# Gate weights and gate logits: one batch or row block in each column quadrant, and transposes in place of stack matmuls

## The chip, the cores and the metric

The kernel runs on one core of a Trainium2 chip. The metric is the time of one execution on the device, in microseconds; for the kernel before, three runs were taken (752.5, 754.86 and 754.75, median 754.75).

## The reference

Dilated and windowed attention over 4 batches of 576 positions gives 2304 tokens of 512 numbers. Then a gated product, and then eight experts, between which a greedy routing divides the tokens:

```python
x = attention(q, k, v)                       # (2304, 512)
x = (((x @ w1) * (x @ w2)) @ w3) @ w_out     # FF = 1024 inside, D = 512 outside
logits = x @ w_gate                          # (2304, 8)
for idx in argsort(-logits.flatten()):       # best (token, expert) pairs first
    # a token that has no place yet goes to the expert, while it has fewer than 288
    ...
for e in range(8):
    out[mask_e] = relu(x[mask_e] @ w1_e[e]) @ w2_e[e]
```

All in float32. Large products are made of three passes over a high and a low part; the logits, on whose order the routing depends, are plain fp32 products.

## The kernel before

**Stages.** The order of the work is written out by hand: Python generators are advanced against each other, and each engine runs its instructions in the order in which they were written. First comes attention, interleaved with the loading of weights. Then `moe(b)` (L398) makes G = (x w1) * (x w2) for each batch b of 576 tokens: in groups of 12 passes (L414 to L416) for 256 or 320 tokens, ScalarE copies one product out (L419) and VectorE multiplies it by the other (L420). G[b] is two tiles of 4 x 128 features by 576 tokens.

**Gate weights.** While `moe(3)` runs, `gates()` (L326) is advanced by one step at each half group. It computes WG = w3 (w_out w_gate), which turns the logits into G times WG, so that the routing need not wait for x. In step c it transposes four 128 x 128 pieces of w_out on TensorE (`turn`, L333; one bank, tag "tr"), ScalarE copies them out, and in the next step four matmuls (`gate`, L343) multiply them by four 128-row pieces of w_gate, one in each column quadrant of the array, that is 32 of its 128 columns. Each quadrant thus holds a quarter of one sum (a partial sum over 128 of 512 features). After every four steps the bank is copied to `ts`, and four stack matmuls (L363) with `ts` as the stationary operand and a 128 x 8 matrix of ones (`C_STK`) as the moving one add the four quadrants and turn the result round; VectorE copies that to `TS` (L364). The bank of tag "rt" exists once, so the next accumulator waits for that copy. Then follows the product with w3 (L372), for which SP fetches the pieces in two sets (`fetch_w3`).

**Logits.** Behind `moe(3)` the logits are made (L803 to L820). In each of eight turns u half a batch (288 tokens, `HT`) is multiplied by WG: 8 matmuls, feature blocks 0 to 3 and then 4 to 7, four column quadrants in turn, each with the sum over two of the eight blocks. ScalarE copies the bank to `lt` (L813), and 18 stack matmuls (L817), as soon as 128 tokens are ready, add the quadrants and turn 128 tokens onto the partitions. One VectorE copy (L820) puts all 2304 x 8 logits into `L`. Ahead of the last stack matmuls one unit of the next product is issued (`next(fill)`).

**Routing and what fills it.** From `L` on the routing (`routing`, L587) is a long chain on VectorE with small matmuls (L744) in between. `filler()` (L1035) puts units of other work on TensorE in between: first the product w3 w_out (`make_w`, L514; a unit is three matmuls, L523 to L525, counted as 680 ns), then x2 (`make_x2`), then the experts. A written-out pace (L1040 to L1046) says how many units stand ahead of each routing step. With block c of x2, from c = 11, `w_split` is called, which splits one expert weight into its high and low part on ScalarE and on VectorE, GpSimd (L122) or a GpSimd DMA; `gsplit` makes GpSimd DMAs too.

Of the kernel before, what the change touches and what calls it, by code (L numbers as in the profile page):

```python
# [9 lines left out]
F32 = mybir.dt.float32  # L10
# [3 lines left out]
AF = mybir.ActivationFunctionType  # L14
# [5 lines left out]
B, S = 4, 576  # L20
N, D, FF, E, CAP = 2304, 512, 1024, 8, 288
QB, KB, NB = 64, 96, 9
HT = 288
HEAD = 256
NC = N // 128
# [4 lines left out]
C_ID, C_STK = 0, 128  # L30
# [55 lines left out]
def body(tc, qk_d, v_d, ke_d, ve_d, msk_d, cst_d, tri_d, w1_d, w2_d, w3_d, wo_d, wg_d, e1_d, e2_d, out):  # L86
    nc = tc.nc
    stacks = {}

    def pool(name, **kw):  # L90
        stacks[name] = ExitStack()
        return stacks[name].enter_context(tc.tile_pool(name=name, bufs=1, **kw))
# [8 lines left out]
    bank = lambda shape, tag, dt=F32: ps.tile(shape, dt, tag=tag, name="ps_" + tag,  # L101
                                              bufs={"ab": 4, "h": 2, "tr": 1, "rt": 1}[tag])
    mm = nc.tensor.matmul
    act = nc.scalar.activation
    dve = nc.vector
# [4 lines left out]
    def slot(i, shape, dt, name):  # L110
        return xp.tile(shape, dt, tag=f"s{i}", name=name, bufs=1)
# [31 lines left out]
    C = cst.tile([128, C_END], F32, name="C")  # L143
    ident = C[:, C_ID:C_ID + 128]
# [148 lines left out]
    got3, narrowed, pre, placed = {}, {}, {}, [0]  # L293
# [28 lines left out]
    TS = pm.tile([128, 512], F32, tag="xr", name="TS", bufs=1)  # L322
    WG = TS[:, :256].rearrange("p (m e) -> p m e", m=8)
    TS = TS[:, 256:].rearrange("p (m e) -> p m e", m=8)

    def gates():  # L326
        wts, accs = [], []
        wg32 = p3.tile([128, 4, 32], F32, name="wg32", bufs=1)
        dve.memset(wg32, 0.0)
        dve.tensor_copy(wg32[:, :, 0:8], wg)  # L330
        dve.memset(TS, 0.0)

        def turn(c):  # L333
            w = narrowed["wo", c // 2]
            t = bank([128, 4, 128], "tr")
            for i in range(4):
                n0 = 512 * (c % 2) + 128 * i
                nc.tensor.transpose(t[:, i, :], w[:, n0:n0 + 128], ident)
            wt = p3.tile([128, 4, 128], F32, tag="wt", name="wt", bufs=1)
            act(wt, t, AF.Copy)  # L340
            wts.append(wt)

        def gate(c):  # L343

            if c % 4 == 0:
                accs.append(bank([128, 4, 128], "rt"))
            wt = wts.pop()
            for i in range(4):
                mm(accs[-1][32 * i:32 * i + 32, c % 4, :], wg32[:, i, :], wt[:, i, :], start=True, stop=True)

        for c in range(9):
            if c:
                gate(c - 1)
            if c in (4, 8):
                ts = p3.tile([128, 4, 128], F32, tag="ts", name="ts", bufs=1)
                act(ts, accs[-1], AF.Copy)
            if c < 8:
                turn(c)
            yield
            if c in (4, 8):  # L360
                o = bank([128, 4, 8], "rt")
                for i in range(4):
                    mm(o[:, i, :], ts[:, i, :], C[:, C_STK:C_STK + 8], start=True, stop=True)  # L363
                dve.tensor_copy(TS[:, c - 4:c, 0:8], o)  # L364
        yield

        acc = bank([128, 2, 128], "rt")
        for a, ms in enumerate(((4, 5, 6, 7), (0, 1, 2, 3))):
            ws = [narrowed["w3", m] for m in ms]
            for k in range(8):  # L370
                for q, w in enumerate(ws):
                    mm(acc[32 * q:32 * q + 32, a, :], TS[:, k, :], w[:, 128 * k:128 * k + 128],  # L372
                       start=(k == 0), stop=(k == 7))
                if k % 2:
                    yield
            if ms[0]:
                fetch_w3(0)
                for _ in range(3):
                    yield
        wt = p3.tile([128, 4, 128], F32, tag="wt", name="wt", bufs=1)[:, :2]  # L380
        act(wt, acc, AF.Copy)
        yield
        t = bank([128, 2, 128], "tr")
        for a in range(2):
            nc.tensor.transpose(t[:, a, :], wt[:, a, :], ident)
        for a in range(2):
            dve.tensor_copy(WG[:, 4 - 4 * a:8 - 4 * a, :], t[:, a, :].rearrange("p (q e) -> p q e", q=4))

    def fetch_w3(m):
        x = p3.tile([128, 2, 1024], F32, tag="S", name="S", bufs=1)  # L390
        for i in range(4):
            fetch(("w3", m + i), x[:, i] if i < 2 else pm.tile([128, 1024], F32, tag="f", name="f", bufs=2))


    G = {}
    L = cst.tile([128, E, NC], F32, name="L")
# [58 lines left out]
    nxt, i = 0, 0  # L455
# [8 lines left out]
    for b in range(B):  # L464
        if b == 3:
            stacks.pop("pa").close()
            p2 = pool("p2")
            p3 = pool("p3")
            for i in range(2):
                x = p2.tile([128, 2, 1024], F32, tag=f"P{i}", name="wo", bufs=1)  # L470
                for n in range(2):
                    fetch(("wo", 2 * i + n), x[:, n])
            fetch_w3(4)
            making_wg = gates()
# [59 lines left out]
    def make_x2():  # L534

        yield from make_w()
        todo = []

        def xout(c, a):
            late = c - (NC - ONE)  # L540
            if late >= 0:
                if not X1:
                    X1.extend(wtile("wb"))
                h, l = [x[:, D * late:D * late + D] for x in X1]
                act(h, a, AF.Copy)
                dve.tensor_tensor(l, a, f32(h), op=OP.subtract)
            r = pm.tile([128, D], F32, tag="xr", name="xr", bufs=1) if late < 1 else rows0[0][:, 3 * D:4 * D]
            act(r, a, AF.Copy)
            nc.scalar.dma_start(x2_d[128 * c:128 * c + 128, :], r)

        def mul(a, g, f, cols):
            h, l = g
            wh, wl = [x[:, f % 2, cols] for x in Wx[f // 2]]
            mm(a, h[:, f, :], wh, start=(f == 0), stop=False)  # L554
            mm(a, h[:, f, :], wl, start=False, stop=False)  # L555
            mm(a, l[:, f, :], wh, start=False, stop=(f == 7))  # L556

        for c in range(NC):
            if c + 2 < NC:
                gsplit(c + 2)  # L560
            if c >= 11:
                w_split()
            if c >= 10:
                w_gather()
            a = bank([128, D], "ab")
            for f in range(8):
                mul(a, GS[c], f, slice(0, D))
                if f == 1 and todo:
                    xout(*todo.pop())
                if f == 2 and c == NC - ONE:  # L570
                    while 0 not in lists:
                        yield 0
                    first_rows()
                yield 680
            todo.append((c, a))
        yield from first_in(lambda: xout(*todo.pop()))
# [223 lines left out]
    route = routing()  # L800
    next(route)
    fill = make_x2()
    lt = slot(3, [128, N], F32, "lt")  # L803
    lo = bank([128, NC, E], "tr")
    c = 0
    for u in range(2 * B + 1):
        if u < 2 * B:
            lg = bank([128, HT], "h")
            for i in range(2):
                for q in range(4):  # L810
                    mm(lg[32 * q:32 * q + 32], WG[:, 4 * i + q, :],
                       G[u // 2][i][:, q, HT * (u % 2):HT * (u % 2) + HT], start=(i == 0), stop=(i == 1))
            act(lt[:, HT * u:HT * u + HT], lg, AF.Copy)  # L813
        else:
            next(fill)
        while u and 128 * (c + 1) <= HT * (u if u == 2 * B else u - 1):
            mm(lo[:, c, :], lt[:, 128 * c:128 * c + 128], C[:, C_STK:C_STK + 8],  # L817
               start=True, stop=True)
            c += 1
    dve.tensor_copy(L, lo.rearrange("p c e -> p e c"))  # L820


    pieces = [(k, n, i) for k in range(E)
              for n, i in ([(1, 0), (1, 1), (2, 0), (2, 1), (1, 2), (2, 2), (1, 3), (2, 3)] if k == 0 else
# [210 lines left out]
    def filler():  # L1035
        yield from fill_x2
        phase[0] = 1
        yield from experts()

    fill_x2, fill = fill, filler()  # L1040
# [67 lines left out]
```

## Time and profile before

| | |
|---|---|
| median of three runs | 754.75 us |
| profiled execution | 752.74 us, span 751.0 us |
| mean granted clock of TensorE | 0.997 |
| TensorE (PE) busy | 720.0 us, 96% |
| weight loads (PEld) | 651.9 us, 87% |
| VectorE (DVE) | 411.0 us, 55% |
| ScalarE (ACT) | 355.7 us, 47% |
| GpSimd (POOL) | 298.8 us, 40% |
| chain that ended last | PE 75%, DVE 9%, issue 6%, ACT 4%, POOL 3% |

Busy times are sums over one execution. A matmul's duration includes its way through the array, and matmuls overlap, so the time of a run of matmuls is the distance of the starts, not the sum of the durations. The chain that ended last goes back from the last instruction to what released it, and so on; its shares tell on which engines the length hangs.

### The profile page before, as it was taken

To read this page: it belongs to the slowest core of one execution; us is meant where nothing else is said; L and a number is where in the kernel's file an instruction comes from. 1 tells how busy PE (TensorE), PEld (TensorE's weight loads), DVE (VectorE), ACT (ScalarE), POOL (GpSimd) and SP (SyncE) were. 2 spreads that over 40 slices of the span, in tenths; PEclk is the share of its full clock that TensorE was granted. 3 is DMA by queue.
4 is the path that set the end of the run, shared out by engine and by line. 5 is a ranking of instruction groups with operands and counts; after the bars stand their busy time and mean duration, and the time that the engine had idled before them with its cause. 6 is when DMAs were issued, how large, how long until landed. Compare 5 with 4: busy or idle time off the path is not lost.

```text
span 751.0 us, 17097 instructions
## 1 busy us (share of the span) xinstructions
PE 720.0 (96%) x6606; PEld 651.9 (87%) x6606; DVE 411.0 (55%) x1360; ACT 355.7 (47%) x833; POOL 298.8 (40%) x357
## 2 busy tenths in 40 slices
PE   5799999999999999999999999999999999999997
PEld 3589999899999988877778787779999999999996
DVE  4987778832322100137787668677788762124321
ACT  5674544444442212422345356426575566665432
POOL 1876211101010002815354456334475574763531
PEclk9999999999999999999999999999999999999999
DMA  8984899832200503011669789976887978996511
GB/s 313 338 251 125 297 348 320 277 108 68 74 28 1 224 2 113 29 36 57 112 82 138 119 123 197 200 224 164 232 235 219 273 213 240 263 272 216 156 33 33
DMA packets 57410, 126.74 MB, mean 169 GB/s; under 512 B 9584, under 2 KB 27120, under 8 KB 54768
## 3 DMA queue, kind: packets, MB, share of 16 engines
q1 hardware_dynamic: 27088, 89.46, 35.7%
q0 software_dynamic: 27648, 31.46, 24.1%
q10 hardware_dynamic: 2592, 4.72, 1.8%
q8 instruction: 52, 0.85, 0.5%
q14 instruction: 30, 0.25, 0.1%
HBM read 87.87 MB, written 15.73 MB: 138 GB/s over the span
## 4 chain that ended last, share of the span: by engine, by line
PE 75%; DVE 9%; issue 6%; ACT 4%; POOL 3%; DMA 2%; SPq 1%; POOLq 0%; DVEq 0%; ACTq 0%
PE ps_ab L414 9%; PE ps_ab L415 8%; PE ps_ab L416 8%; PE ps_ab L554 4%; PE ps_ab L555 3%; PE ps_ab L556 3%; PE ps_h L935 3%; PE ps_h L936 3%; PE ps_h L937 3%; PE ps_ab L959 3%; PE ps_ab L961 3%; PE ps_ab L960 3%; PE ps_rt L744 2%; PE ps_rt L223 2%; PE ps_ab L523 2%
## 5 line engine op out<-in xcount | busy, mean ns | idle before, releaser
L420 DVE TENSOR_TENSOR g<-a,ps_ab 128x256 f32<-128x256 f32 (+1 forms) x64 | 28.9, 452 | 137.4 <-PE ps_ab L416 131.7
L204 POOL TENSOR_TENSOR p<-p,sm 128x384 f32<-128x384 f32 x36 | 38.9, 1080 | 151.2 <-ACT p L197 75.9
L414 PE MATMUL ps_ab<-x,wah 128*128 128x256 f32 (+1 forms) x256 | 78.7, 307 | 0.0
L414 PE MATMUL ps_ab<-x,wbh 128*128 128x256 f32 (+1 forms) x256 | 78.5, 307 | 0.0
L439 POOL DMA_DIRECT2D wbl<-g x40 | 52.2, 1706 | 63.2 <-ACT wbl L437 53.2
L416 PE MATMUL ps_ab<-x,wal 128*128 128x256 f32 (+1 forms) x256 | 76.2, 298 | 0.0
L415 PE MATMUL ps_ab<-x,wah 128*128 128x256 f32 (+1 forms) x256 | 76.2, 298 | 0.0
L959 PE MATMUL ps_ab<-hh,w 128*128 128x288 f32 x248 | 75.9, 306 | 0.0
L416 PE MATMUL ps_ab<-x,wbl 128*128 128x256 f32 (+1 forms) x256 | 75.7, 296 | 0.0
L415 PE MATMUL ps_ab<-x,wbh 128*128 128x256 f32 (+1 forms) x256 | 75.7, 296 | 0.0
L961 PE MATMUL ps_ab<-hh,w 128*128 128x288 f32 x248 | 73.0, 294 | 0.0
L960 PE MATMUL ps_ab<-hl,w 128*128 128x288 f32 x248 | 72.9, 294 | 0.0
L419 ACT ACTIVATE a<-ps_ab 128x256 f32<-128x256 f32 (+1 forms) x64 | 26.1, 408 | 97.3 <-PE ps_ab L416 97.3
L197 ACT ACTIVATE p<-p,sm 128x96 f32<-128x96 f32 x144 | 52.0, 363 | 37.1 <-DVE sm L190 37.1
L948 DVE SCALAR_TENSOR_TENSOR hl<-ps_h,hh 128x288 fp32r<-128x288 f32 x62 | 28.2, 455 | 68.7 <-ACT hh L947 68.7
L947 ACT ACTIVATE hh<-ps_h 128x288 fp32r<-128x288 f32 x62 | 25.5, 412 | 84.5 <-PE ps_h L937 84.5
L554 PE MATMUL ps_ab<-Wx,wbh 128*128 128x512 f32 x144 | 60.2, 418 | 0.0
L555 PE MATMUL ps_ab<-Wx,wbh 128*128 128x512 f32 x144 | 56.8, 394 | 0.0
L556 PE MATMUL ps_ab<-Wx,wbl 128*128 128x512 f32 x144 | 56.7, 394 | 0.0
L414 PEld LDWEIGHTS ps_ab<-x,wah 128*128 128x128 f32 x256 | 49.0, 191 | 2.6 <-issue 1.0
L414 PEld LDWEIGHTS ps_ab<-x,wbh 128*128 128x128 f32 x256 | 48.4, 189 | 3.1 <-issue 1.0
L416 PEld LDWEIGHTS ps_ab<-x,wal 128*128 128x128 f32 x256 | 49.0, 192 | 0.0
(272 smaller groups left out, 2123.7 us busy)
## 6 DMA issues: line engine op xcount, KB each, us to landing
w<-w_dram SPq DMA_DIRECT2D x16, 1024.0 KB, 8.1
est<-e_dram SPq DMA_DIRECT2D x31, 512.0 KB, 5.0
qk<-qk_dram SPq DMA_DIRECT2D x36, 320.0 KB, 5.1
yt<-e_dram SPq DMA_DIRECT2D x22, 512.0 KB, 5.2
wbl<-g POOLq DMA_DIRECT2D x32, 256.0 KB, 6.3
v<-v_dram SPq DMA_DIRECT2D x36, 192.0 KB, 4.3
kept<-f SPq DMA_DIRECT2D x12, 512.0 KB, 4.0
w<-est POOLq DMA_DIRECT2D x12, 512.0 KB, 6.5
```

Source lines behind the costliest of these rows:

```text
L197: act(p[:, i, :], p[:, i, :], AF.Exp, bias=sm[:, 1, i:i + 1], scale=-1.0, accum_out=sm[:, 2, i:i + 1])
L204: nc.gpsimd.tensor_tensor(p, p, sm[:, 3, :, None].to_broadcast([128, 4, KB]), op=OP.mult)
L414: mm(a, wh[:, k, fs], xh[:, k, ts], start=(k == 0), stop=False)
L415: mm(a, wh[:, k, fs], xl[:, k, ts], start=False, stop=False)
L416: mm(a, wl[:, k, fs], xh[:, k, ts], start=False, stop=(k == 3))
L439: nc.gpsimd.dma_start(x, src, accum_op=OP.add)
L554: mm(a, h[:, f, :], wh, start=(f == 0), stop=False)
L555: mm(a, h[:, f, :], wl, start=False, stop=False)
L556: mm(a, l[:, f, :], wh, start=False, stop=(f == 7))
L959: mm(y, wh[:, f % 2, ds_], h, start=(f == 0), stop=False)
L960: mm(y, wh[:, f % 2, ds_], l, start=False, stop=False)
L961: mm(y, wl[:, f % 2, ds_], h, start=False, stop=(f == end))
```

## The change

The gate weights: one accumulator holds all eight row blocks. In step r (group g, feature block i) the four transposed pieces are of four row blocks and one feature block; quadrant q of the array takes row block q, and the sum over the four feature blocks is made by accumulating over four steps. At the end there are one copy of 256 columns, two plain transposes and one VectorE copy. The logits: quadrant b takes batch b, and the sum over the eight feature blocks is accumulated in place, for tokens 0 to 287 of all batches and then 288 to 575. ScalarE copies each quadrant to its place in `lt`, which is now 128 x 640; batches 1 and 3 stand 64 columns further right, so that five 128 x 128 transposes turn all tokens as the routing wants them. GpSimd fills the columns left over with zeros, three units of the next product stand ahead of the transposes, and five VectorE copies go to `L`.

```diff
@@ -324,44 +324,40 @@
     TS = TS[:, 256:].rearrange("p (m e) -> p m e", m=8)
 
     def gates():
-        wts, accs = [], []
         wg32 = p3.tile([128, 4, 32], F32, name="wg32", bufs=1)
         dve.memset(wg32, 0.0)
         dve.tensor_copy(wg32[:, :, 0:8], wg)
         dve.memset(TS, 0.0)
-
-        def turn(c):
-            w = narrowed["wo", c // 2]
+        acc = bank([128, 2, 128], "rt")
+
+        def turn(r):
+            g, i = divmod(r, 4)
             t = bank([128, 4, 128], "tr")
-            for i in range(4):
-                n0 = 512 * (c % 2) + 128 * i
-                nc.tensor.transpose(t[:, i, :], w[:, n0:n0 + 128], ident)
+            for q in range(4):
+                w = narrowed["wo", 2 * g + q // 2]
+                n0 = 512 * (q % 2) + 128 * i
+                nc.tensor.transpose(t[:, q, :], w[:, n0:n0 + 128], ident)
             wt = p3.tile([128, 4, 128], F32, tag="wt", name="wt", bufs=1)
             act(wt, t, AF.Copy)
-            wts.append(wt)
-
-        def gate(c):
-
-            if c % 4 == 0:
-                accs.append(bank([128, 4, 128], "rt"))
-            wt = wts.pop()
-            for i in range(4):
-                mm(accs[-1][32 * i:32 * i + 32, c % 4, :], wg32[:, i, :], wt[:, i, :], start=True, stop=True)
-
-        for c in range(9):
-            if c:
-                gate(c - 1)
-            if c in (4, 8):
-                ts = p3.tile([128, 4, 128], F32, tag="ts", name="ts", bufs=1)
-                act(ts, accs[-1], AF.Copy)
-            if c < 8:
-                turn(c)
+            return wt
+
+        def gate(r, wt):
+            g, i = divmod(r, 4)
+            for q in range(4):
+                mm(acc[32 * q:32 * q + 32, g, :], wg32[:, i, :], wt[:, q, :], start=(i == 0), stop=(i == 3))
+
+        for r in range(8):
+            wt = turn(r)
             yield
-            if c in (4, 8):
-                o = bank([128, 4, 8], "rt")
-                for i in range(4):
-                    mm(o[:, i, :], ts[:, i, :], C[:, C_STK:C_STK + 8], start=True, stop=True)
-                dve.tensor_copy(TS[:, c - 4:c, 0:8], o)
+            gate(r, wt)
+        ts = p3.tile([128, 4, 128], F32, tag="ts", name="ts", bufs=1)[:, :2]
+        act(ts, acc, AF.Copy)
+        yield
+        t = bank([128, 2, 128], "tr")
+        for g in range(2):
+            nc.tensor.transpose(t[:, g, :], ts[:, g, :], ident)
+        dve.tensor_copy(TS.rearrange("p (g q) e -> p g q e", g=2)[:, :, :, 0:8],
+                        t.rearrange("p g (q e) -> p g q e", q=4)[:, :, :, 0:8])
         yield
 
         acc = bank([128, 2, 128], "rt")
@@ -800,25 +796,30 @@
     route = routing()
     next(route)
     fill = make_x2()
-    lt = slot(3, [128, N], F32, "lt")
-    lo = bank([128, NC, E], "tr")
-    c = 0
-    for u in range(2 * B + 1):
-        if u < 2 * B:
-            lg = bank([128, HT], "h")
-            for i in range(2):
-                for q in range(4):
-                    mm(lg[32 * q:32 * q + 32], WG[:, 4 * i + q, :],
-                       G[u // 2][i][:, q, HT * (u % 2):HT * (u % 2) + HT], start=(i == 0), stop=(i == 1))
-            act(lt[:, HT * u:HT * u + HT], lg, AF.Copy)
-        else:
-            next(fill)
-        while u and 128 * (c + 1) <= HT * (u if u == 2 * B else u - 1):
-            mm(lo[:, c, :], lt[:, 128 * c:128 * c + 128], C[:, C_STK:C_STK + 8],
-               start=True, stop=True)
-            c += 1
-    dve.tensor_copy(L, lo.rearrange("p c e -> p e c"))
-
+    lt = slot(3, [128, S + 64], F32, "lt")
+    for b in range(B):
+        nc.gpsimd.memset(lt[32 * b:32 * b + 32, 0:64] if b % 2 else lt[32 * b:32 * b + 32, S:], 0.0)
+    for u in range(2):
+        lg = bank([128, HT], "h")
+        for f in range(8):
+            for b in range(B):
+                mm(lg[32 * b:32 * b + 32], WG[:, f, :], G[b][f // 4][:, f % 4, HT * u:HT * u + HT],
+                   start=(f == 0), stop=(f == 7))
+        for b in range(B):
+            c0 = 64 * (b % 2) + HT * u
+            act(lt[32 * b:32 * b + 32, c0:c0 + HT], lg[32 * b:32 * b + 32], AF.Copy)
+    for _ in range(3):
+        next(fill)
+    lo, le = bank([128, 4, 128], "tr"), bank([128, 128], "rt")
+    for j in range(5):
+        nc.tensor.transpose(lo[:, j, :] if j < 4 else le, lt[:, 128 * j:128 * j + 128], ident)
+    Lb = L.rearrange("p e (b c) -> p b c e", b=2)
+    lo = lo.rearrange("p j (b x) -> p b j x", b=2)
+    le = le.rearrange("p (b x) -> p b x", b=2)
+    for p, c, x in ((slice(0, 128), slice(0, 4), lo[:, :, :, 0:8]), (slice(0, 128), slice(5, 8), lo[:, :, 1:4, 32:40]),
+                    (slice(64, 128), 4, lo[:, :, 0, 32:40]), (slice(0, 64), 4, le[:, :, 0:8]),
+                    (slice(0, 128), 8, le[:, :, 32:40])):
+        dve.tensor_copy(Lb[p, :, c], x[p])
 
     pieces = [(k, n, i) for k in range(E)
               for n, i in ([(1, 0), (1, 1), (2, 0), (2, 1), (1, 2), (2, 2), (1, 3), (2, 3)] if k == 0 else
```

## Rows read from the trace of the kernel before

**Rows 1.** Busy time by stretch: PE, PEld, DVE, ACT, POOL (instructions), PEclk, DMA share, GB/s.

```profile
250.00:275.00 25.00, 24.62 (x248) 21.91 (x250) 3.10 (x10) 7.45 (x16) 0.00 (x0) 1.00 0.27 107
315.00:329.00 14.00, 14.00 (x169) 8.70 (x169) 1.16 (x11) 4.33 (x9) 5.37 (x8) 1.00 0.20 73
329.00:620.00 291.00, 283.09 (x2348) 246.39 (x2348) 218.82 (x724) 148.43 (x222) 146.81 (x163) 0.99 0.77 167
```

**Rows 2.** The chain of waits over the logits: start us, us, what.

```profile
315.09 3.05 PE ps_h L811 x48
318.14 0.54 PE ps_tr L817 x4
318.68 1.11 PE ps_h L811 x16
...
323.09 0.77 PE ps_tr L817 x6
...
327.95 1.02 PE ps_tr L817 x10
...
329.77 0.23 PE ps_ab L523
```

**Rows 3.** Groups of instructions, 200 to 420 us: busy us, mean ns, idle before.

```profile
L338 PE MATMUL ps_tr<-C,wo 128*128 128x128 f32 x32 | 5.2, 285 | 0.0
...
L813 ACT ACTIVATE lt<-ps_h 128x288 f32<-128x288 f32 x8 | 3.3, 412 | 7.8 <-PE ps_h L811 7.8
...
L364 DVE COPY TS<-ps_rt 128x32 f32<-128x32 f32 x2 | 0.4, 192 | 0.6 <-PE ps_rt L363 0.6
```

**Rows 4.** Timeline of TensorE in the gate weights: start us, us, instruction.

```profile
250.71 0.60 PE L338 MATMUL ps_tr<-C,wo 128*128 128x128 f32 x4
251.07 0.36 PE L414 MATMUL ps_ab<-x,wbh 128*128 128x256 f32 x1
...
260.54 0.36 PE L414 MATMUL ps_ab<-x,wbh 128*128 128x256 f32 x1
...
264.15 0.36 PE L414 MATMUL ps_ab<-x,wah 128*128 128x256 f32 x1
...
266.53 0.36 PE L414 MATMUL ps_ab<-x,wbh 128*128 128x256 f32 x1
...
272.39 0.96 PE L363 MATMUL ps_rt<-C,ts 128*128 128x8 f32 x8
273.20 0.36 PE L414 MATMUL ps_ab<-x,wah 128*128 128x256 f32 x1
```

**Rows 5.** Timeline of the other engines around the logits.

```profile
315.20 0.49 DVE L420 TENSOR_TENSOR g<-a,ps_ab 128x320 f32<-128x320 f32 x1 [3.03 <-PE ps_ab L416]
...
317.60 2.77 POOL L122 TENSOR_TENSOR wbl<-f,wbh 128x256 fp32r<-128x256 f32 x4
...
329.00 0.31 DVE L820 COPY L<-ps_tr 128x144 f32<-128x144 f32 x1 [12.65 <-PE ps_tr L817]
...
334.55 0.69 DVE L512 TENSOR_TENSOR Wx<-ps_ab,Wx 128x512 fp32r<-128x512 f32 x1 [2.21 <-ACT Wx L511]
```

**Rows 6.** Routing: timelines, one stretch, and TensorE's longest wait (total, times, longest).

```profile
477.83 2.29 DVE L749 SCALAR_TENSOR_TENSOR r_u<-r_any,r_u 128x18 f32<-128x18 f32 x1
...
476.85 3.89 POOL L122 TENSOR_TENSOR wal<-est,wah 128x256 fp32r<-128x256 f32 x4
...
481.57 0.61 PE L744 MATMUL ps_rt<-r_Gt,r_CR 128*128 128x40 bf16 x18 [1.72 <-DVE r_Gt L733]
...
484.00:486.00 2.00, 2.00 (x9) 1.71 (x9) 1.24 (x3) 0.21 (x1) 0.00 (x0) 0.50 0.77 279
...
PE ps_rt L744 <- DVE r_Gt L733: 4.4, 5, 1.7
```

**Rows 7.** DMA issues from 244.6 to 244.9, then to 245.3: KB, median us to landing.

```profile
wo<-kept SPq DMA_DIRECT2D x1, 512.0 KB, 3.3
wo<-kept SPq DMA_DIRECT2D x2, 512.0 KB, 3.8
```

## The prediction

> **What bounds the kernel now.** I read the stretches of the run first (busy time of each engine), then the chain of waits around the two places of the change, then the timelines there, then the waits of the stage behind. In the stage of the gate weights TensorE is busy 24.62 of 25 us, in the stage of the logits 14.00 of 14, in the whole routing stage 283.09 of 291 [rows 1]. No other engine comes near it, and the DMA share is high only in the routing stage. So what TensorE no longer does in these two stages should bring the end forward, unless the routing stage gives it back: there 7.9 us are idle, and they are waits for VectorE, the longest kind 4.4 us in 5 waits [rows 6].
>
> **Logits, before.** The chain is TensorE alone, and each row is a run of passes (an fp32 product is two passes, a transpose one). The 64 logit matmuls are 128 passes: the first 48 take 3.05 us, then five blocks of 16 take 1.11 each, so 3.05 + 5.55 = 8.60 us. The 18 stack matmuls are 36 passes: five rows of four at 0.54, one of six at 0.77, one of ten at 1.02, so 4.49 us. Together 13.09 us [rows 2].
>
> **Logits, after.** Still 64 matmuls of 32 columns over 288, and still the four column quadrants in turn; only what a quadrant holds differs. Unbroken they should run at the rate of the unbroken row: 128 x 3.05 / 48 = 8.13 us. (At the rate of the broken blocks, 1.11 / 16, it is 8.88: the upper end that I keep; the lower end is 8.13 too, as no row with 288 columns is faster.) I take 8.13, since the new stream is not broken. Five transposes replace the stack. Four of the same shape start at 250.71 and the next matmul at 251.07, so 0.09 each and 0.45 for five [rows 4]. The upper end for one is its whole duration, 0.285 [rows 3], if nothing overlaps. Before the change the same four ran overlapped, so I take 0.09. Sum 8.58, saved 4.51 us.
>
> What of this lies on a wait? The last element-wise product of the batch before is written from 315.20 to 315.69 [rows 5]. The first matmul of the new order that reads it is the 32nd (20th, if the whole tile is waited for), 2.4 us or more behind the start: covered. ScalarE copies eight pieces as before, 0.412 each as the length is the same [rows 3], but the last four now come together at the end: 4 x 0.412 and about 0.23 to be released is 1.9 us. In that time TensorE has three units of the weight product where there was one, 9 x 0.23 = 2.07 us [rows 2]. So the transposes wait for nothing, by a margin of 0.2; if ScalarE is one copy late, 0.2 us is lost. GpSimd gets four fills of 32 x 64. It is busy with a split until 317.60 + 2.77 = 320.4 [rows 5], five us ahead of the transposes. Even at the split's own 0.7 us each (a much larger operand) they end at 323.2. Behind them stands only the next split, far later. Nobody waits.
>
> VectorE makes five small copies where there was one. A copy of 32 columns out of PSUM takes 0.192 [rows 3], one of 144 takes 0.308 [rows 5], so about 1 ns a column on 0.16: lengths 64, 48 and three of 16 give 0.23 + 0.21 + 3 x 0.18 = 0.97 us against 0.31. The routing chain so starts 0.66 us later behind TensorE's logits than it did. The cover is the 2.21 us for which VectorE idles ahead of its first evacuation at 334.55 [rows 5]. I cost it at nothing; without the cover it is 0.66.
>
> Two units of the product (2 x 0.69 us) move ahead of the routing. The total is the same, so the sum doesn't change, but from here on every routing step stands against work that is two units further on. That is the rival below.
>
> **Gate weights.** Both versions do 32 transposes and 32 gate matmuls in the same eight steps, with the same number of yields (ten) ahead of the w3 product. What goes are two groups of four stack matmuls, each eight passes, and one wait. An ordinary step lasts from 264.15 to 266.53, 2.38 us; the step with the first stack group lasts from 260.54 to 264.15, 3.61: 1.23 us go, the wait of TensorE for VectorE's copy included, as the single bank of this tag now stays with one accumulator. The second group takes from 272.39 to 273.20, 0.81 us. In its place come two transposes, 2 x 0.09 = 0.18 [rows 4]. Saved 1.23 + 0.81 - 0.18 = 1.86 us. The lower end has the two transposes at 0.285, 1.47 us. One need is new: the first step now reads two of the four w_out pieces instead of one. The first landed 3.3 us after its issue; the median of the first two is 3.8, so the second took 4.3. Issued before 245.3, it is there by 249.6, and TensorE comes to it at 250.71 [rows 7]: 1.1 us to spare. What stalls next is the wait for the second set of w3 pieces, which follows from this stage's own reads and moves with them.
>
> **Sum.** 4.51 + 1.86 = 6.37 us. The profiled execution took 752.74 (span 751.0, the rest lies around it): 746.4 by that. It is 2.0 under the median of the three runs, 754.75; against the median the sum gives 748.4, and that is my forecast.
>
> What speaks against it most is a rule. The transposes' row shows durations of 0.285 us [rows 3] and starts 0.09 apart [rows 4]. The Trainium skill, "TensorE: Matmul & The Clock Gate", Part 4: PE-mode transpose, gives about 275 ns for one in a kernel, mostly access latency. If that were time on the engine, seven would cost 1.93 us by the page. The duration agrees with the trace; that it is paid in full does not.
>
> **The rivals.**
>
> *Transposes paid in full.* Seven at the row's 0.285 are 2.0 us instead of 0.63: saved 5.0, time 749.8. For: nothing but the duration; against: the starts. 0.04.
>
> *Collisions in the routing fall otherwise.* At 477.83 a VectorE operation of 18 columns takes 2.29 us, while GpSimd's split runs from 476.85. TensorE then waits 1.72 for the comparison at 481.57, and after that its granted clock is 0.50 from 484 to 486, the lower level [rows 6]. These splits belong to fixed units of the product, and two units' shift moves them by 1.4 us against the routing steps. Two more such hits cost 2 x 1.7 us, and a fall of the clock like that one costs about as much again as a wait: 3 to 4 us back, 752. Fewer hits give 3.4 (the wait and the clock): 745. For: the waits are there now, and what falls beside what is decided by this shift alone; against: it isn't plain which way, since each split is issued anyway and holds VectorE somewhere. 0.13 for worse, 0.10 for better. The Trainium skill, "SBUF — State Buffer", Who interferes with whom, says that VectorE and GpSimd share one pair of ports which the first to start holds for its whole instruction. The trace agrees, with the 2.29 us; the prices above don't need it.
>
> *The quadrants stop overlapping.* A pass of 512 columns at full width takes 0.23 us, so one of 288 at full width about 0.13, and a quadrant pass takes 0.064 only because quadrants overlap [rows 2]. If four quadrants that stream from four different batches didn't overlap, 128 passes would take 16.6 us instead of 8.13. Then 8.4 us come on and 6.4 go: 2.0 slower, 756.8. It decides from a pass of (8.13 + 6.37) / 128 = 0.113 us. Against: the order of quadrants is unchanged, and only the address of the stream differs. 0.04.
>
> *TensorE isn't the bound behind.* If the routing stage went by its transfers (share 0.77) [rows 1], an earlier start would be used up there, and the change would not do what it says: about 754. Against: the waits of TensorE in that stage, whose longest kind stands in [rows 6], are all for VectorE, none for a DMA, and the transfers are issued by the same chain, so they start earlier too. 0.04.
>
> **How the numbers follow.** 0.65 for the forecast, whose own bounds are +0.75 (logits at the broken rate) + 0.66 (routing start) on one side and the 2.0 between the median and the profiled run on the other: 746.4 to 749.8. The range takes in a collision more at the top, 749.8 + 1.7 + 0.4 = 751.9, and at the bottom the fall of the clock gone, 746.4 - 1.7 = 744.7. A measurement of this kernel can tell about 0.3%, 2.3 us, from no change. Faster by more than that: 0.65 + 0.10 + 0.04 and half of the worse collisions, 0.85. Same: the other half and the transfers, 0.10. Slower: 0.05.
>
> **What would show it.** The logit stage runs from its first matmul to its fifth transpose in about 8.6 us plus three units of product at 2.1, and no TensorE idle before the transposes. The step that held the first stack group is as long as its neighbours, 2.4. The first routing product waits for nothing. Wrong would be: quadrant passes above 0.07, transposes 0.2 or more apart, a wait of TensorE at the first transpose of the gate stage for the w_out pieces, or an idle time in the routing stage that is 3 us off the 7.9 of before.

## The result, and the profile after

The changed kernel takes 747.38 us (median of five runs, 745.47 to 748.67) beside 752.50 for the kernel before on the same chip. The ratio is 0.9904, interval 0.9878 to 0.9931: 0.7 to 1.2% faster. A second measurement on another occasion gave 746.12 beside 753.60, ratio 0.9895 (0.9862 to 0.9928). The forecast was 748.4, or 6.37 us off, which is 0.85%: right in the direction and the size. Between the medians lie 5.1 us here and 7.5 in the second measurement. The level of 748.4 rests on the median of three runs before, 754.75; five runs had 752.50, so that the level came out within 1.0 us, while the saving of 6.37 lies 1.3 above the one and 1.1 below the other.

The profiled execution has a span of 745.6 us, 5.4 less. First the busy time by stretch, as in [rows 1]: the gate stage from its first transpose to the first w3 product, the logit stage to its last transpose, and the routing stage.

```profile
252.76:274.90 22.14, 22.14 (x220) 19.38 (x218) 2.24 (x6) 6.54 (x14) 0.00 (x0) 1.00 0.28 112
314.00:324.55 10.55, 10.55 (x143) 6.27 (x143) 1.16 (x11) 4.25 (x9) 5.90 (x12) 1.00 0.29 97
324.55:614.00 289.45, 281.02 (x2337) 244.92 (x2336) 218.13 (x726) 148.57 (x221) 145.88 (x162) 0.99 0.78 168
```

The gate stage took from 250.71 to 274.80 before, 24.09 us; it is 1.95 shorter. The logit stage is 10.55 us with three units of the next product in it. TensorE idles 8.4 us in the routing stage, where it idled 7.9. One thing is no part of the change: the gate stage begins at 252.76 and began at 250.71, with the same instructions ahead of it. That start lies between 250.2 and 254.6 in all the kernels below, so a part of the difference between two single executions is no work of the edits. The granted clock of the first 50 us, 1.00 before and 0.83 after, doesn't explain it: the repeated changed kernel has 1.00 there and begins the stage at 254.6. Nor is the wait of 0.87 us for w3 pieces part of the change: it stands between the two stages before, is missing here and is back in the repeated kernel.

The chain of waits over the logits answers to [rows 2], with two rows of the timeline for the transposes:

```profile
314.08 7.90 PE ps_h L806 x128
```

```profile
324.09 0.60 PE L815 MATMUL ps_tr<-C,lt 128*128 128x128 f32 x4
324.53 0.27 PE L815 MATMUL ps_rt<-C,lt 128*128 128x128 f32 x1
324.55 0.48 PE L519 MATMUL ps_ab<-wah,wbh 128*128 128x512 f32 x1
```

All 128 passes are one unbroken run, 0.062 each. The transposes take from 324.09 to 324.55, 0.46 us, and carry no wait. So 8.36 us of logits stand against 13.09 before.

The chain in the gate stage: every gate step is now alike, and two transposes stand where the last stack group stood [rows 4].

```profile
259.52 0.36 PE ps_rt L347 x8
...
261.89 0.36 PE ps_rt L347 x8
...
264.26 0.36 PE ps_rt L347 x8
...
273.34 0.22 PE ps_tr L358 x2
```

The starts of the steps are 2.37 us apart, also where the step of 3.61 was.

Behind the logits there is a new wait, in the chain ahead of the first routing product:

```profile
327.89 0.84 ACT r_CR L711
...
328.76 0.61 ACT Wx L507
...
329.39 0.69 DVE Wx L508
...
330.59 0.65 DVE r_ki L719
...
331.26 0.68 DVE r_kf L720
...
331.96 0.67 DVE r_u L724
...
332.65 1.40 DVE r_Gt L729
```

```profile
334.19 0.61 PE L740 MATMUL ps_rt<-r_Gt,r_CR 128*128 128x40 bf16 x18 [1.19 <-DVE r_Gt L729]
```

The same place before, on VectorE and on TensorE (the evacuation at 334.55 is in [rows 5]):

```profile
332.16 0.18 DVE L724 CAST r_kf<-r_ki 128x36 f32<-128x36 int32 x1
...
337.12 0.62 PE L744 MATMUL ps_rt<-r_Gt,r_CR 128*128 128x40 bf16 x18
```

Before, the first evacuation (`Wx`) stood behind the routing's integer steps (`r_ki`, `r_kf`); now it stands ahead of them. VectorE waits for ScalarE there, and the split that GpSimd starts right behind it, at 330.44, stretches steps of 0.18 us to some 0.67. TensorE waits 1.19 us.

A second new wait comes later, at 453.82:

```profile
453.82 0.70 PE L740 MATMUL ps_rt<-r_Gt,r_CR 128*128 128x40 bf16 x18 [1.90 <-DVE r_lf L673]
```

All five profiles with three units ahead, here and below, have it with 1.90 or 1.91 us, and none of the nine with one unit. Before, GpSimd's split fell one routing step later there, and the wait was shorter:

```profile
459.75 0.61 PE L744 MATMUL ps_rt<-r_Gt,r_CR 128*128 128x40 bf16 x18 [0.86 <-DVE r_Gt L733]
```

Other waits are shorter in return: the whole idle time of TensorE behind the logits is 8.4 us here and 7.7 in the repeated changed kernel, beside 7.9 before.

### The profile page after: what moved, and what is told of

The parts are those of the page before. It is cut to its first block, busy times and chain, and to the rows that moved or that the text cites. A ratio compares the mean times of both kernels' runs of the same rounds, so it can differ in the third digit from the quotient of the medians.

```text
span 745.6 us, 17007 instructions
## 1 busy us (share of the span) xinstructions
PE 712.7 (96%) x6561; PEld 646.9 (87%) x6561; DVE 410.8 (55%) x1363; ACT 355.3 (48%) x832; POOL 300.4 (40%) x361
## 4 chain that ended last, share of the span: by engine, by line
PE 80%; issue 6%; DVE 6%; ACT 3%; POOL 2%; DMA 1%; SPq 1%; POOLq 0%; DVEq 0%
PE ps_ab L410 10%; PE ps_ab L411 9%; PE ps_ab L412 9%; PE ps_ab L550 4%; PE ps_ab L552 4%; PE ps_ab L551 4%; PE ps_h L936 3%; PE ps_ab L960 3%; PE ps_h L938 3%; PE ps_h L937 3%; PE ps_ab L962 3%; PE ps_ab L961 3%; PE ps_rt L740 3%; PE ps_rt L223 3%; PE ps_h L176 2%
## 5 line engine op out<-in xcount | busy, mean ns | idle before, releaser
L410 PEld LDWEIGHTS ps_ab<-x,wbh 128*128 128x128 f32 x256 | 49.0, 191 | 3.1 <-issue 1.2
L411 PEld LDWEIGHTS ps_ab<-x,wbh 128*128 128x128 f32 x256 | 49.1, 192 | 0.0
```

Of the source, the lines that this page charges most:

```text
L410: mm(a, wh[:, k, fs], xh[:, k, ts], start=(k == 0), stop=False)
L411: mm(a, wh[:, k, fs], xl[:, k, ts], start=False, stop=False)
```

## The experiments

**One half at a time.** The kernel before with the gate weights' part of the diff alone, and with the logits' part alone.

> Only the gate weights are changed, the logits are as before. Theory (the time saved is TensorE's own, stage by stage): from the first transpose of the gate stage to the first w3 product 22.1 us, as in the changed kernel (24.09 before), and the kernel 1.9 us faster than before, 0.25%. The one of two waits for the second set of w3 pieces that TensorE had before (0.87 us) is chance of the transfers and may or may not be there. Rival (what the gate stage saves is given back, as the second set of w3 pieces is fetched at its own pace): stage 22.1, but the wait for the pieces grows by up to 1.9 us and the kernel's time is that of before.

> Only the logits are changed, the gate weights are as before. Theory: the logit stage, units of the next product taken off, takes 8.4 us (13.2 before), the first routing product waits some 1.2 us as in the changed kernel, and the kernel is 3.5 to 4.5 us faster than before. Rival (the gain came from how the routing's collisions happened to fall and from the transfers): the logit stage is shorter, but the time is less than 2 us off that of before.

Gates alone: ratio 0.9981 (0.9956 to 1.0005). The chain shows the same stage as the changed kernel; from its first transposes, at 251.28 in the chain, to the first w3 product are 22.1 us:

```profile
269.72 0.36 PE ps_rt L347 x8
271.70 0.22 PE ps_tr L358 x2
273.35 0.57 PE ps_rt L368 x16
```

The wait for the w3 pieces was there, 0.9 us, as before and no longer: the rival's growth didn't come. The time itself is too close to no change to tell. Logits alone: ratio 0.9939 (0.9922 to 0.9956), 4.6 us; the 128 passes take 7.90 us again, and the 1.2 us wait at the first routing product is there too. The two ratios multiply to 0.992, inside the interval of the whole change.

**One unit ahead of the transposes.**

```diff
-    for _ in range(3):
-        next(fill)
+    next(fill)
```

> The changed kernel with one unit of the next product ahead of the five transposes in place of three. Theory: ScalarE's last four copies end 1.9 us behind the last logit product, one unit covers 0.8 us of that, so TensorE waits 1.1 us at the first transpose; in return the first evacuation stands behind the routing's integer steps again, as in the kernel before, and the 1.19 us wait at the first routing product is gone or under 0.4. The sum of both waits is then the same, and so is the time, within 1 us of the changed kernel. Rival A (the two units' shift costs in the whole routing stage, not at its first product): faster than the changed kernel by 2 us or more. Rival B (the wait at the first product comes from VectorE's four added copies, not from where the evacuation stands): the wait of 1.19 us stays and the time is 1.1 us longer.

Two rows of its TensorE timeline at the transposes and at the first routing product:

```profile
322.87 0.44 PE L814 MATMUL ps_tr<-C,lt 128*128 128x128 f32 x2 [0.66 <-ACT lt L810]
...
331.47 0.62 PE L740 MATMUL ps_rt<-r_Gt,r_CR 128*128 128x40 bf16 x18
```

The first transposes start before the last copies, so only 0.66 us is waited, and the 1.19 at the first product is gone: so the two units' shift made that wait, not the four added copies. Yet the ratio is 0.9946 (0.9920 to 0.9972), no better than the change, so rival A fell as well. Its profile shows where some of it went, at the first expert's products and in the stretch behind (columns as in [rows 1]):

```profile
493.97 1.27 PE L885 MATMUL ps_h<-dg,rows 96*128 96x96 f32 x4 [3.17 <-DMA rows<-x_d,li]
```

```profile
494.00:502.00 8.00, 8.00 (x35) 7.74 (x36) 2.86 (x12) 0.60 (x1) 0.00 (x0) 0.50 0.82 287
```

TensorE reaches the first expert before the gathered rows have landed, waits 3.17 us, and runs at the lower of its two clocks for eight us behind that. The wait took the place of others, as the idle time behind the logits is 7.8 us in all; what the profile has more of is the lower clock.

**Two copiers.** The copies of batches 1 and 3 to `lt` by VectorE, one unit ahead.

```diff
-            act(lt[32 * b:32 * b + 32, c0:c0 + HT], lg[32 * b:32 * b + 32], AF.Copy)
+            if b % 2:
+                dve.tensor_copy(lt[32 * b:32 * b + 32, c0:c0 + HT], lg[32 * b:32 * b + 32])
+            else:
+                act(lt[32 * b:32 * b + 32, c0:c0 + HT], lg[32 * b:32 * b + 32], AF.Copy)
```

> The changed kernel with the copies of batches 1 and 3 to lt moved from ScalarE to VectorE, and one unit of the next product ahead of the transposes in place of three. Theory: the last copies end about 1.1 us behind the last logit product, one unit covers 0.8, so TensorE waits 0.3 us or less at the transposes; the evacuation stands where it stood before, so the first routing product waits under 0.4 us; 0.5 to 1.2 us faster than the changed kernel. Rival (the wait at the first routing product is set by GpSimd's split, which holds VectorE wherever it falls): it waits about 1 us all the same, and the time is that of the changed kernel.

Ratio 0.9906 (0.9881 to 0.9931), that of the change. The copies did not run side by side, as VectorE's timeline shows:

```profile
323.06 0.45 DVE L811 COPY lt<-ps_h 32x288 f32<-32x288 f32 x1 [2.47 <-ACT lt L813]
323.98 0.46 DVE L811 COPY lt<-ps_h 32x288 f32<-32x288 f32 x1 [0.47 <-ACT lt L813]
```

Each waits for the other engine's copy, so four take as long as four in a row, and TensorE waits 0.83 at the transposes, not 0.3 or less. The first routing product waits for nothing, which refutes the rival. Why copies of different quadrants are ordered was not settled.

**What the stack cost.** The kernel before with its stack matmuls in one run at the end.

```diff
-        while u and 128 * (c + 1) <= HT * (u if u == 2 * B else u - 1):
-            mm(lo[:, c, :], lt[:, 128 * c:128 * c + 128], C[:, C_STK:C_STK + 8],
-               start=True, stop=True)
-            c += 1
+    for c in range(NC):
+        mm(lo[:, c, :], lt[:, 128 * c:128 * c + 128], C[:, C_STK:C_STK + 8],
+           start=True, stop=True)
```

> The kernel before, with its 18 logit stack matmuls in one run behind all 64 logit products in place of seven groups between them. Theory (going back and forth between the quadrant products and the full-width stack costs time by itself): the products take 7.9 us as one run (8.60 before), the 36 stack passes 0.102 us each as in the run of ten, 3.7 us (4.49 before), so the stage is 11.6 us and one unit, 1.5 us shorter than before, and 3.2 us of the change's 4.7 are the stack itself. Rival (the alternation is free, the passes are what costs): the stage stays at 13.1 us and one unit.

Its chain:

```profile
313.88 7.90 PE ps_h L811 x128
...
322.67 4.55 PE ps_tr L817 x36
```

The products gain what the theory said (8.60 to 7.90). The 4.55 us of the stack passes are not all of one kind: the granted clock falls in the middle of them, though TensorE waits for nothing there (columns PE, PEld, PEclk, DMA share, GB/s, stack passes alone):

```profile
322.67:325.66 2.99, 2.99 (x30) 2.99 (x29) 1.00 0.01 4
325.79:327.07 1.28, 1.28 (x8) 1.28 (x7) 0.50 0.00 0
```

At 1.00 the passes start 0.11 us apart, at 0.50 they start 0.21 apart. So 36 passes at the higher clock would take some 4.0 us (an estimate from these starts), the stage 11.9 and one unit, and alternating cost about 1.2 us of the 13.09, near the 1.5 of the theory; the passes themselves cost the other 4.0. One unit stands between the two rows of the chain. The Trainium skill, "TensorEngine Tiling (Array Packing)", Key Properties, says that a change of the tiling mode drains TensorE; the unbroken run fits that, and by the estimate it is the small part here, 1.2 of the 4.7 us that the logits saved.

**The order of quadrants.** The changed kernel with the loops over f and b exchanged.

```diff
-        for f in range(8):
-            for b in range(B):
+        for b in range(B):
+            for f in range(8):
```

> The changed kernel with the two inner loops of the logits exchanged: all eight feature blocks of a batch in a row, so that 16 passes in a row fall in one quadrant. Theory (a pass takes 0.062 us because neighbours in different quadrants overlap): a pass then takes 0.12 us or more (288 columns at the 0.23 us for 512 columns are 0.129), the 128 passes 15 to 17 us, 7 to 9 us longer. Rival (a pass is bound by its issue or its weight load, not by the array): 7.9 us as before the exchange. One in between, about 11 us, if only the two passes of one product must follow each other.

```profile
313.14 24.58 PE ps_h L806 x128
```

0.192 us a pass, three times the rotating order and more than I expected, at a granted clock of 1.00; the kernel took 762.6 in its one execution, 9.6 more than the kernel before beside it. The price named for the rival of lost overlap was too low. That neighbours come from different batches does no harm, as the changed kernel's 0.062 shows; a row of passes in one quadrant does. Here such neighbours also add to one accumulator, and no run parts the two.

**The price of a transpose.** Each of the five made four times.

```diff
-    for j in range(5):
+    for j in [j for j in range(5) for _ in range(4)]:
```

> The changed kernel with each of the five logit transposes made four times, the same result each time. Theory (a transpose costs its start-to-start distance, 0.09 us): 20 transposes take 1.85 us, 1.4 us longer. Rival (it costs its duration of 0.27 us once it is not hidden beside products): 5.4 us.

```profile
325.92 1.91 PE L815 MATMUL ps_tr<-C,lt 128*128 128x128 f32 x16
327.66 0.60 PE L815 MATMUL ps_rt<-C,lt 128*128 128x128 f32 x4
```

The first sixteen take 1.74 us by their starts, 0.11 each; all twenty 2.1, to the next product at 328.02. That is a little over the 1.85 of the theory, and far from the duration of 0.27 each.

**Two batches to a copy.** Batches 0, 2, 1, 3 in the quadrants, one copy for 64 partitions, one unit ahead.

```diff
-        for b in range(B):
-            c0 = 64 * (b % 2) + HT * u
-            act(lt[32 * b:32 * b + 32, c0:c0 + HT], lg[32 * b:32 * b + 32], AF.Copy)
+        for o in range(2):
+            c0 = 64 * o + HT * u
+            act(lt[64 * o:64 * o + 64, c0:c0 + HT], lg[64 * o:64 * o + 64], AF.Copy)
```

> The changed kernel with batches 0, 2, 1, 3 in quadrants 0 to 3, so that the two batches that stand at the same columns of lt lie on 64 neighbouring partitions and one ScalarE copy takes both (two copies of 64 x 288 for each half in place of four of 32 x 288), two fills in place of four, and one unit of the next product ahead of the transposes in place of three. Theory: the last copies end 0.23 + 2 x 0.41 = 1.05 us behind the last product, one unit covers 0.8 of that, TensorE waits 0.3 us or less at the transposes; with the units taken off the logit stage is 0.3 us longer than in the changed kernel, and the first routing product, which waited 1.19 us there, waits under 0.4 as with one unit: 0.8 us faster in these two stages together. Rival: a copy of 64 partitions takes as long as two of 32, and TensorE waits about 1 us at the transposes.

ScalarE's row in the timed repetition of this kernel:

```profile
323.37 0.82 ACT L811 ACTIVATE lt<-ps_h 64x288 f32<-64x288 f32 x2 [3.04 <-PE ps_h L807]
```

Two copies take 0.82 as four took 1.65, the first routing product waits for nothing, and from the first logit product to the first routing product it takes 17.5 us where the changed kernel takes 20.2 with two units more (18.8 without them). 1.3 us saved, yet the kernel's first execution took 751.23: it has 3.37 us of wait for the gathered rows, and the lower clock behind it.

**Where it goes.** The last four were timed side by side: the changed kernel again, the two batches to a copy, and two versions of that with the gather eased.

> The changed kernel once more, unaltered, beside the others of this call. Theory (5.1 to 7.2 us come from TensorE's own time in the two stages, the rest of the differences between runs from the routing stage): 0.8 to 1.0% faster than before, and again 22.1 us from the first transpose to the first w3 product and 8.4 us of logits without the units. Rival (the first result leaned on lucky runs): under 0.6%.

> The version with two batches to a copy and one unit ahead of the transposes, timed. Theory (what it saved up to the first routing product, 1.3 us, brings TensorE to the first expert's gathered rows before they have landed; the wait of 3.4 us and the lower clock behind it take it back): no faster than the changed kernel, 747 to 751, with a wider spread. Rival (the wait for the gathered rows was chance in one look): 1 us or more faster than the changed kernel.

> As the version with two batches to a copy, but the first expert's gather reads rows of an expert weight, which lie in memory from the start, in place of the rows of x2, so it needn't wait until x2's block 15 is written (this leaves the first expert's input wrong; the work is the same). Theory: no wait of TensorE for the gathered rows and no lower clock behind it, 4 to 8 us faster than the version with two batches to a copy, 741 to 745. Rival A (the gather's own way from issue to landing, some 5 us, is what is late, not the write of x2 ahead of it): the wait stays at 2 us or more and the time too. Rival B (a collision of VectorE and GpSimd takes the place of the wait): the wait goes, the time falls by less than 2 us.

```diff
-in_=x2_d[:128 * (NC - ONE), :],
+in_=e1_d.rearrange("o p (h f) -> (o p h) f", h=2)[:128 * (NC - ONE), :],
```

> As the version with two batches to a copy, with the last three blocks of x2 in place of two brought to the first expert by one-hot products, so that the gather needs blocks 0 to 14 only and is issued one block (5.5 us of products) earlier. It adds eight matmuls of 288 columns, 8 x 0.13 = 1.05 us. Theory: the wait for the gathered rows goes, with the lower clock behind it; 3 to 7 us faster than the version with two batches to a copy, 742 to 746, and so 2 us or more faster than the changed kernel. Rival: the added splits and comparisons on VectorE, or the added pair of weight tiles, make TensorE wait as much as it saves; 746 or more.

```diff
-ONE, GATHER_F = 2, 2
+ONE, GATHER_F = 3, 2
...
-                if not X1:
-                    X1.extend(wtile("wb"))
-                h, l = [x[:, D * late:D * late + D] for x in X1]
+                if late % 2 == 0:
+                    X1.append(wtile("wb"))
+                h, l = [x[:, D * (late % 2):D * (late % 2) + D] for x in X1[late // 2]]
```

The third block takes a second pair of weight tiles, and the late products read `X1[i // 2]`.

| | median us | ratio to before | interval |
|---|---|---|---|
| changed kernel again | 746.12 | 0.9895 | 0.9862 to 0.9928 |
| two batches to a copy | 747.69 | 0.9916 | 0.9885 to 0.9947 |
| gather from other rows | 744.54 | 0.9882 | 0.9854 to 0.9911 |
| three late blocks | 747.35 | 0.9920 | 0.9892 to 0.9948 |

The changed kernel repeats, with 22.2 us of gate stage and 10.5 of logit stage. The two batches to a copy are no faster, as the theory had it, but its cause was not in the profile: in that execution the gathered rows had landed, and TensorE had waited just ahead of them for VectorE instead:

```profile
494.33 0.61 PE L740 MATMUL ps_rt<-r_Gt,r_CR 128*128 128x40 bf16 x18 [1.93 <-DVE r_Gt L729]
```

It had also waited 2.42 us for VectorE at 477.97.

With the gather from other rows the median is 3.1 us lower than with two batches to a copy; the profile has no wait for the rows and none at 494, but one of 2.35 us for VectorE twenty us earlier, where the other has its 2.42. As neither profile has a wait for the rows, they don't show that the difference comes from the gather. It is between the theory (4 to 8) and rival B (under 2), and the intervals overlap. With three late blocks the wait is gone too, and the time did not fall, against the theory; its profile has the wait for VectorE at the earlier place:

```profile
475.61 0.61 PE L740 MATMUL ps_rt<-r_Gt,r_CR 128*128 128x40 bf16 x18 [2.04 <-DVE r_Gt L729]
```

So in the routing stage one of several waits ends last, and which one differs between executions of one kernel. They replace each other: the idle time of TensorE behind the logits is 7.2 to 9.1 us in all fourteen profiles. What differs more is the lower clock, and why it falls in one execution and not in another stays open; no version here is shown to beat the changed kernel.

## Why the prediction was right

*Logits, 8.58 us forecast, 8.36 measured.* The rate of the unbroken row held and was a little better (0.062 against 0.064 a pass), and five transposes cost 0.46 against 0.45. Saved 4.7, forecast 4.51.

*The covers.* Three units hid the four copies: the last ended at 323.69 and the transposes started at 324.09. GpSimd's four fills took 0.69 together and ended at 320.0. VectorE's five copies took 0.85, forecast 0.97. No TensorE wait for the last product of G.

*Gate weights, 1.86 forecast, 1.95 measured*, in the changed kernel, and about as much with the gates alone. The two transposes took 0.22 where I had 0.18. The second piece of w_out was there in time.

*The step that failed: the start of the routing, costed at nothing.* I feared VectorE's later start (at most 0.66) and named the idle time ahead of the evacuation as its cover. The measured wait is 1.19 us, and it has another cause: with two units moved ahead, that evacuation itself goes ahead of the routing's integer steps, so the cover was no longer idle time behind them but a wait in front of them, and GpSimd's split followed it. One unit in place of three took the wait away. The shift was in the prediction as a rival, for the later collisions, but it was not followed to the first place where it acts. Nor was it followed to the later step with the wait of 1.90. That the sum held all the same was not the work of the cover: other waits became shorter by about as much, and that was luck.

*The sum.* The two stages gave 4.73 + 1.95 = 6.68 us, beside 6.37 forecast. The medians differ by 5.1 and 7.5; what lies between those and 6.68 is within the spread of the profiles behind the logits, and its cause isn't shown.

*The rivals.* Transposes in full: refuted, 0.11. The Trainium skill's 275 ns ("TensorE: Matmul & The Clock Gate", Part 4: PE-mode transpose) is the duration that the trace shows and not what a transpose costs in a run of them. Overlap lost: refuted for this order, and real for another. TensorE not the bound behind: no, but it stands nearer than I said. I wrote that no wait of TensorE there is for a DMA; in the kernel before that was so, and in six of the kernels above there is one of 0.6 to 3.4 us. Collisions: they stayed. From the last transpose or stack pass to the end, the kernels with one unit ahead take 419.9 to 425.9 us in the profiles and those with three 418.6 to 422.7, to which two units, 1.4 us, are to be added. The routing stage neither paid for the change nor took it back beyond that spread. The four longest, 424.1 to 425.7 with the two units added, are those whose clock stood at the lower level for six us or more between 492 and 510. So in these profiles the price of a collision lies more in the clock than in the waits.

## What to carry to other kernels

When small outputs share the array by quadrants, let a quadrant hold a whole sum and accumulate it in place: adding the quadrants afterwards cost 4.5 us here for 36 passes, and five transposes 0.46. Keep the quadrants in turn, since a pass cost three times as much where its neighbours had the same quadrant and accumulator. And when filler work is moved ahead of a chain, follow every instruction that the filler issues on other engines to its new place, above all the first one.

## What was not expected of the hardware

Sixteen passes in a row in one quadrant cost 0.192 us each. That is more than the 0.13 estimated for a full-width pass of 288 columns from the 512-column passes of [rows 2], which are passes over high and low parts and not plain fp32.

A wait of TensorE of 3.2 us for a transfer was followed by eight us at a granted clock of 0.50, where waits of 1.2 to 1.9 us for VectorE in the routing stage of the repeated changed kernel were followed by none. The length alone doesn't settle it: in the kernel before the lower clock came behind a wait of 1.72 [rows 6]. The wait at 453.82 in the changed kernel shows it best. First the stretch behind it in the first profile, then the wait and the stretch in the repeated kernel's (columns of the stretches as in [rows 1]):

```profile
454.00:456.00 2.00, 2.00 (x21) 1.71 (x18) 1.30 (x6) 1.97 (x3) 1.19 (x2) 0.51 0.88 281
```

```profile
457.31 0.61 PE L740 MATMUL ps_rt<-r_Gt,r_CR 128*128 128x40 bf16 x18 [1.91 <-DVE r_lf L673]
```

```profile
457.00:459.00 2.00, 1.70 (x23) 1.49 (x23) 1.32 (x9) 1.97 (x3) 0.71 (x1) 1.00 1.02 282
```

The same wait in the same kernel was followed by the lower clock once and not the other time. And with the stack passes in one row the clock fell with no wait ahead of it at all: TensorE had been busy, for 3 us with passes of eight columns.
